# Last output tile stored in two halves on two queues; the first chunk's operand steps put on odd units of the last attention heads

## The chip, the cores and the metric

The program runs on one core of a Trainium2 chip. The metric is the device time of one execution in microseconds (us). The engines of the core are TensorE (PE, with its weight loads PEld), VectorE (DVE), ScalarE (ACT), GpSimd (POOL) and SyncE (SP, which here issues nearly all DMAs). Each has its own instruction queue, taken in order; engines meet only at semaphores.

## The reference

```python
q_bits = (q @ proj > 0); k_bits = (k @ proj > 0)          # 6 bits: one bucket per row
scores = where(bucket(q) == bucket(k), 0.125 * q @ k.T, -1e9)
attn = exp(scores - max) / (sum + 1e-9)                    # [4, 8, 768, 768]
x = (attn @ v).transpose(0, 2, 1, 3).reshape(3072, 512)
h = x @ w_in                                               # [3072, 2048]
g = where(h >= 1, h, where(h <= -1, 0, (h + 1) ** 2 / 4))
out = g @ w_out                                            # [3072, 512] f32
```

## The kernel before

All matrix products are done in pieces of reduced precision: an operand x is split into a high part (a cast to fp32r) and a low part (x minus the high part), and three products (high x high, high x low, low x high) are summed. So for every operand there is a cast and a subtraction somewhere.

**Attention** runs 384 units g = 0 to 383: 32 heads, for each two halves of 384 query columns, for each six key blocks j = g % 6. In unit g, `attention` (the loop at its end) issues in this order:

- `s_unit(g)`: two matmuls into a score tile `s` (L350, L351), two exponentials on ACT (L359 the high part `ph`, L364 the full value). The full value goes back into `s`, or for j = 0 and 3 into an SBUF tile `pf`.
- `max_red`: in odd units up to 359, the maximum of a score tile of a later head, on DVE (L314, `nm<-smax`).
- `lo_unit(g-1)`: the low part `pl` of the unit before, on DVE (`pl<-s,ph`) or, for j = 0 and 3, on POOL (`pl<-pf,ph`). All subtractions go through one helper, L39.
- `pv_unit(g-4)`: three matmuls into `o` (L383, L384, L385). L385 is the one that reads `pl`. The key blocks are taken in the order `PV_ORDER` = 1, 2, 0, 4, 5, 3, so the first one of a half reads block 1: unit 370 reads the `pl` of unit 367, unit 376 that of unit 373, unit 358 that of unit 355.
- `max_mm`: in even units up to 358, two matmuls into `smax` (L310). `smax` is one tile, so they wait until the reduction of the pair before has read it.
- the tasks that were put at g in a table (`at(g, fn, ...)`), in the order in which they were put there.

Tasks of the last four heads (units 336 to 383, `g0 = 336`) prepare the feed-forward part. Those of this case:

- `XMaker.make` makes the operand of the first token chunk for four column tiles ct = 0 to 3, in four steps: part 0, L668, `raw = er * sv + raw` on DVE; part 1, L671, `raw = raw * r` on DVE; part 2, L673, the cast to the high part on DVE (`t<-raw`); part 3 the low part on POOL (L39, `t<-raw,t`). The tile `t` of part 2 and 3 lies in SBUF, as `raw` and `er` do.
- `late[n]` casts a staged weight on DVE (L89, `t<-wsq`) and one unit later subtracts on POOL (L39, `t<-wsq,t`); casts stand in units 354, 366, 371 and 376 among others.

**The feed-forward part** follows (`ffn`): products for the hidden values h (L928, L1023) and for the output y (L791), with ACT and DVE for the activation. `flush` copies a finished output tile of 128 x 512 from PSUM to SBUF and stores it by DMA. The last six tiles of the program are stored at the end, one after the other; the very last copy is on DVE (L778), the others on ACT (L780), and all six DMAs are issued by SP (L781).

The order of all instructions is written out by hand; nothing reorders them.

Of the kernel before, what the change touches and what calls it, by code (L numbers as in the profile page):

```python
# [22 lines left out]
P = 128  # L23
# [586 lines left out]
HM = DM // 2  # L610
# [78 lines left out]
def ffn(ctx, tc, wpair, woh, wol, xm, xa, xb, areas, wst, wq, wc, out, prep, post, staged):  # L689
# [3 lines left out]
    nc = tc.nc  # L693
# [73 lines left out]
    ys = {}  # L767

    def flush(c, m):
        r0 = c * CH + m * P  # L770
        n = (c % 2 * 3 + m) % 4 if c > 1 else 0
        if c == 2 * B - 2:
            ot = pcs.rearrange("p k n -> p (k n)")[:, m * DM:(m + 1) * DM]
        else:
            ot = (xp.tile([P, DM], F32, name="ot", bufs=2) if n < 2
                  else sflat[:, (n - 2) * DM:(n - 1) * DM])
        if c == 2 * B - 2 and m == CH // P - 1:
            nc.vector.tensor_copy(out=ot, in_=ys[c][m])  # L778
        else:
            nc.scalar.copy(out=ot, in_=ys[c][m])  # L780
        nc.sync.dma_start(out=out[r0:r0 + P, :], in_=ot)  # L781

    queue = []
# [1 line left out]
    def queue_out(c, f, g, first, last):  # L785

        def mm(m, k):
            if first and m == 0 and k == 0:
                ys[c] = [ps_y.tile([P, 512], F32, name="y") for _ in range(CH // P)]
            g_, w = ((g[0], woh[f]), (g[0], wol[f]), (g[1], woh[f]))[k]  # L790
            nc.tensor.matmul(out=ys[c][m], lhsT=g_[:, m * P:(m + 1) * P], rhs=w, start=(first and k == 0),  # L791
                             stop=(last and k == 2))
            if last and k == 2:
                flush(c, m)
        queue.extend((mm, (m, k)) for m in range(CH // P) for k in range(3))
# [139 lines left out]
    for ct in range(NCT):  # L935
        for part in range(4):
            n = (1, 2, 3, 5)[ct] + (0, 0, 0, 2)[part]
# [4 lines left out]
    for i in range(4):  # L942
        n = 19 + 3 * i
        w_plan(i, n, n + 2, n + 2, (n + 2, n + 2), (n + 3, n + 3), n + 3)
    for i in range(4, NFT // 2):
        n = N1 + NBLK * (i - 4)
# [60 lines left out]
    for k in range(NK):  # L1007
# [10 lines left out]
        n = 0  # L1018
# [12 lines left out]
        elif s == 2:  # L1031
            src, c, f = ps, 0, 0
        elif s == 3:
            nc.vector.tensor_tensor(out=cv, in0=ps, in1=cm, op=ALU.add)
        elif s == 4:
            nc.vector.tensor_tensor(out=cm, in0=ps, in1=cv, op=ALU.add)
            src, c, f = cm, 1, 1
        elif s == 5:
            nc.vector.tensor_tensor(out=cv, in0=cv, in1=ps, op=ALU.subtract)
            src, c, f = cv, 1, 0  # L1040
        else:
            nc.vector.tensor_tensor(out=cu, in0=ps, in1=cu, op=ALU.add)
            src, c, f = cu, 0, 1
# [24 lines left out]
def lsh_attn_ffn(ctx: ExitStack, tc: tile.TileContext, qk, v, pj, cv, w_in, w_out, out):  # L1068
    nc = tc.nc
# [42 lines left out]
    def at(g, fn, *a):  # L1112
        tasks[g].append((fn, a))
# [50 lines left out]
    for ct in range(NCT):  # L1164
        at(g0 + 4 + 4 * ct, load_er, 0, ct)
        at(gx + 4 + 4 * ct, load_er, 1, ct)
        for part, n in enumerate((14, 18, 19, 20)):
            at(g0 + n + 6 * ct, xm.make, 0, ct, part, *xa, (nc.vector, nc.gpsimd))

    for i in (2, 3):  # L1170
# [9 lines left out]
    for i in range(2, NFT):  # L1180
        n = i + NFT - NW1
# [71 lines left out]
```

## Time and profile before

| what | value |
|---|---|
| median of 3 runs | 985.68 us (984.98 to 985.96) |
| profiled execution: time, span | 986.29 us, 984.5 us |
| busy PE, DVE, ACT, POOL | 98%, 81%, 69%, 35% of the span |
| last matmul ends, last copy ends | 980.60, 981.32 us |
| attention's last units (from unit 350) | from 432.30 us; feed-forward from 468.15 us |
| granted TensorE clock | 1.00 in all windows read here |

The span runs from the first to the last instruction of the profiled execution; 1.8 us of its own time lie around it. Times below are microseconds from the start of the span, and durations of single instructions are from that one execution.

### The profile page before, as it was taken

To read this page: it belongs to the slowest core of one execution; us is meant where nothing else is said; L and a number is where in the kernel's file an instruction comes from. 1 tells how busy PE (TensorE), PEld (TensorE's weight loads), DVE (VectorE), ACT (ScalarE), POOL (GpSimd) and SP (SyncE) were. 2 spreads that over 40 slices of the span, in tenths; PEclk is the share of its full clock that TensorE was granted. 3 is DMA by queue.
4 is the path that set the end of the run, shared out by engine and by line. 5 is a ranking of instruction groups with operands and counts; after the bars stand their busy time and mean duration, and the time that the engine had idled before them with its cause. 6 is when DMAs were issued, how large, how long until landed. Compare 5 with 4: busy or idle time off the path is not lost.

```text
span 984.5 us, 15564 instructions
## 1 busy us (share of the span) xinstructions
PE 968.2 (98%) x5047; PEld 891.9 (91%) x5047; DVE 799.5 (81%) x1359; ACT 679.3 (69%) x1483; POOL 342.1 (35%) x411
## 2 busy tenths in 40 slices
PE   7999999999999999999999999999999999999998
PEld 5789999999999999999999998888988888988896
DVE  8789999999999999988798887887876777655554
ACT  6779888998999888988655556555564545554444
POOL 7666777778877777766100000000000000000000
PEclk8999999999999999999999999999999999999999
DMA  6654667766656667554496478977449554454431
GB/s 174 177 154 101 174 179 191 199 173 168 177 140 180 173 187 191 136 146 124 127 286 217 118 245 271 299 239 210 118 151 245 147 185 116 130 168 118 115 93 64
DMA packets 94712, 167.55 MB, mean 170 GB/s; under 512 B 13940, under 2 KB 51432, under 8 KB 94632
## 3 DMA queue, kind: packets, MB, share of 16 engines
q1 hardware_dynamic: 94408, 166.56, 59.3%
q8 instruction: 40, 0.66, 0.3%
q14 instruction: 40, 0.33, 0.1%
q10 hardware_dynamic: 224, 0.00, 0.0%
HBM read 106.13 MB, written 33.87 MB: 142 GB/s over the span
## 4 chain that ended last, share of the span: by engine, by line
PE 90%; DVE 5%; ACT 2%; DMA 1%; issue 1%; SPq 0%; DVEq 0%
PE y L791 27%; PE h L1023 18%; PE smax L310 7%; PE h L928 7%; PE o L385 6%; PE s L351 6%; PE o L384 6%; PE o L383 6%; PE s L350 6%; PE o L204 2%; DVE nm L314 2%; DMA vraw<-in_v_dram 1%; DVE pl L39 1%; DMA t<-te 1%; ACT ph L359 0%
## 5 line engine op out<-in xcount | busy, mean ns | idle before, releaser
L359 ACT ACTIVATE ph<-s 128x384 fp32r<-128x384 f32 x380 | 188.1, 495 | 47.5 <-PE s L351 41.8
L314 DVE TENSOR_REDUCE nm<-smax 128x1 f32<-128x768 f32 x189 | 178.9, 947 | 16.2 <-PE smax L310 14.5
L39 POOL TENSOR_TENSOR pl<-pf,ph 128x384 fp32r<-128x384 f32 x128 | 139.0, 1089 | 90.4 <-ACT pf L364 90.1
L756 DVE SCALAR_TENSOR_TENSOR t<-t 128x384 f32<-128x384 f32 x128 | 71.3, 557 | 101.7 <-ACT z L751 101.5
L39 DVE TENSOR_TENSOR pl<-s,ph 128x384 fp32r<-128x384 f32 x256 | 135.5, 544 | 10.2 <-ACT s L364 9.4
L350 PE MATMUL s<-t 128*128 128x384 f32 x384 | 132.6, 345 | 0.0
L385 PE MATMUL o<-pl,va 128*128 128x386 f32 x384 | 130.6, 340 | 0.4 <-DVE pl L39 0.4
L384 PE MATMUL o<-ph,vb 128*128 128x386 f32 x384 | 130.6, 340 | 0.0
L351 PE MATMUL s<-t 128*128 128x384 f32 x384 | 130.3, 339 | 0.2 <-DMA t<-te 0.2
L383 PE MATMUL o<-ph,va 128*128 128x386 f32 x384 | 130.2, 339 | 0.1
L364 ACT ACTIVATE s<-s 128x384 f32<-128x384 f32 x252 | 124.9, 496 | 0.0
L791 PE MATMUL y<-t,ghi 128*128 128x512 f32 x384 | 124.6, 395 | 0.0
L310 PE MATMUL smax<-t 128*128 128x384 f32 x378 | 104.0, 356 | 6.6 <-DVE nm L314 6.1
L750 ACT ACTIVATE t<-h,mh 128x384 f32<-128x384 f32 x56 | 32.6, 581 | 84.4 <-PE h L928 44.3
L310 PEld LDWEIGHTS smax<-t 128*128 128x128 f32 x378 | 65.5, 191 | 23.5 <-DVE nm L314 23.0
L761 ACT CAST ghi<-z 128x384 fp32r<-128x384 f32 x129 | 65.1, 505 | 30.1 <-DVE z L757 26.3
L751 ACT ACTIVATE z<-t,m 128x384 f32<-128x384 f32 x128 | 79.0, 617 | 4.2
L1023 PE MATMUL h<-wbig,t 128*128 128x384 f32 x399 | 81.4, 336 | 0.0
L791 PEld LDWEIGHTS y<-t,ghi 128*128 128x128 f32 x384 | 71.3, 188 | 11.1 <-ACT ghi L761 0.3
L1023 PEld LDWEIGHTS h<-wbig,t 128*128 128x128 f32 x399 | 71.6, 188 | 5.3
L791 PE MATMUL y<-t,glo 128*128 128x512 f32 x192 | 76.0, 396 | 0.0
L791 PE MATMUL y<-woh,glo 128*128 128x512 f32 x192 | 75.7, 394 | 0.2
(181 smaller groups left out, 2092.0 us busy)
## 6 DMA issues: line engine op xcount, KB each, us to landing
t<-wc SPq DMA_DIRECT2D x92, 256.0 KB
t<-t SPq DMA_DIRECT2D x60, 384.0 KB
wraw<-wc SPq DMA_DIRECT2D x76, 256.0 KB
raw<-in_qk_dram SPq DMA_DIRECT2D x15, 768.0 KB
wraw<-in_w_in_dram SPq DMA_DIRECT2D x16, 512.0 KB
wraw<-in_w_out_dram SPq DMA_DIRECT2D x16, 512.0 KB
t<-ed SPq DMA_DIRECT2D x36, 192.0 KB
xd<-xs SPq DMA_DIRECT2D x32, 192.5 KB
```

The source lines that it names most:

```text
L39: eng.tensor_tensor(out=out, in0=a, in1=b, op=ALU.subtract)
L310: nc.tensor.matmul(out=smax[hd][:, hf, 0:HS], lhsT=t2[:, 0, h, i * P:(i + 1) * P], rhs=t2[:, 1, h, hf * HS:(hf + 1) * HS], start=True, sto ...
L314: nc.vector.tensor_reduce(out=nmp(hd)[:, i:i + 1], in_=smax[hd][:, :, 0:HS], axis=AX.XY, op=ALU.max, negate=True)
L350: nc.tensor.matmul(out=ps[:, 0:HS], lhsT=t1[:, 1, h, ks], rhs=t1[:, 0, h, sl], start=True, stop=False)
L351: nc.tensor.matmul(out=ps[:, 0:HS], lhsT=t2[:, 1, h, ks], rhs=t2[:, 0, h, sl], start=False, stop=True)
L359: nc.scalar.activation(out=ph[:, 0:HS], in_=ps[:, 0:HS], func=AF.Exp, scale=SCALE)
L364: nc.scalar.activation(out=pf, in_=ps[:, 0:HS], func=AF.Exp, scale=SCALE)
L383: nc.tensor.matmul(out=o, lhsT=wa, rhs=ph, start=(jj == 0), stop=False)
L384: nc.tensor.matmul(out=o, lhsT=wb, rhs=ph, start=False, stop=False)
L385: nc.tensor.matmul(out=o, lhsT=wa, rhs=pl, start=False, stop=(jj == NJ - 1))
L791: nc.tensor.matmul(out=ys[c][m], lhsT=g_[:, m * P:(m + 1) * P], rhs=w, start=(first and k == 0), stop=(last and k == 2))
L1023: nc.tensor.matmul(out=ps, lhsT=w[:, cs], rhs=x, start=(n == 0 and s not in (2, 3, 6)), stop=(n == 5), skip_group_check=True)
```

## The change

```diff
         if c == 2 * B - 2 and m == CH // P - 1:
-            nc.vector.tensor_copy(out=ot, in_=ys[c][m])
-        else:
-            nc.scalar.copy(out=ot, in_=ys[c][m])
+
+            for n, q in enumerate((nc.sync, nc.scalar)):
+                sl = slice(n * HM, (n + 1) * HM)
+                nc.vector.tensor_copy(out=ot[:, sl], in_=ys[c][m][:, sl])
+                q.dma_start(out=out[r0:r0 + P, sl], in_=ot[:, sl])
+            return
+        nc.scalar.copy(out=ot, in_=ys[c][m])
         nc.sync.dma_start(out=out[r0:r0 + P, :], in_=ot)
...
-        for part, n in enumerate((14, 18, 19, 20)):
+        for part, n in enumerate((13, 17, 19, 21) if ct else (15, 17, 19, 21)):
             at(g0 + n + 6 * ct, xm.make, 0, ct, part, *xa, (nc.vector, nc.gpsimd))
```

HM is 256. The first edit replaces the last copy of 512 columns by two of 256, and its store by two, the second issued by ACT. The second edit moves steps between units:

| ct | parts 0, 1, 2, 3 before | now |
|---|---|---|
| 0 | 350, 354, 355, 356 | 351, 353, 355, 357 |
| 1 | 356, 360, 361, 362 | 355, 359, 361, 363 |
| 2 | 362, 366, 367, 368 | 361, 365, 367, 369 |
| 3 | 368, 372, 373, 374 | 367, 371, 373, 375 |

On DVE in units 353 to 357 (here `raw` and `t2_1_78` are the operand's tiles, `wsq` the staged weight; lines with + are of the changed kernel, lines with - of the kernel before, which alone has the rows so marked):

```order
+L671 TENSOR_TENSOR raw_5434<-raw_5434,t2_1_78 128x384
 L39 TENSOR_TENSOR pl_3_164<-s_5637,ph_3_157 128x384
 L89 CAST t1_1_75<-wsq_5593 128x512
-L671 TENSOR_TENSOR raw_5434<-raw_5434,t2_1_78 128x384
-L314 TENSOR_REDUCE nm_5586<-smax_5661 128x1
+L314 TENSOR_REDUCE nm_5586<-smax_5662 128x1
 L673 CAST t2_1_78<-raw_5434 128x384
+L668 SCALAR_TENSOR_TENSOR raw_5434<-t2_1_78,xsv0_5435,raw_5434 128x384
 L39 TENSOR_TENSOR pl_5_166<-s_5666,ph_5_159 128x384
-L668 SCALAR_TENSOR_TENSOR raw_5434<-t2_1_78,xsv0_5435,raw_5434 128x384
-L314 TENSOR_REDUCE nm_5586<-smax_5687 128x1
+L314 TENSOR_REDUCE nm_5586<-smax_5688 128x1
```

Part 1 of ct 0 has moved ahead of the low part of unit 353 and of the weight's cast; part 0 of ct 1 now stands right behind part 2 of ct 0 and ahead of `pl_5_166`, the low part of unit 355. Between the two reductions stand the same three operations as before.

On DVE in units 365 to 369 (`pl_1_162` is the low part of unit 365, `pl_3_164` that of unit 367, `pl_4_165` that of unit 368):

```order
+L671 TENSOR_TENSOR raw_5434<-raw_5434,t2_1_78 128x384
 L39 TENSOR_TENSOR pl_1_162<-s_5788,ph_1_155 128x384
 L89 CAST t1_2_76<-wsq_5749 128x512
-L671 TENSOR_TENSOR raw_5434<-raw_5434,t2_1_78 128x384
 L673 CAST t2_1_78<-raw_5434 128x384
+L668 SCALAR_TENSOR_TENSOR raw_5434<-t2_1_78,xsv0_5435,raw_5434 128x384
 L39 TENSOR_TENSOR pl_3_164<-s_5815,ph_3_157 128x384
-L668 SCALAR_TENSOR_TENSOR raw_5434<-t2_1_78,xsv0_5435,raw_5434 128x384
-L39 TENSOR_TENSOR pl_4_165<-s_5826,ph_4_158 128x384
+L39 TENSOR_TENSOR pl_4_165<-s_5827,ph_4_158 128x384
```

Part 1 of ct 2 goes ahead of the low part of unit 365, and part 0 of ct 3 goes ahead of the low part of unit 367, which it followed before.

## Rows read from the trace of the kernel before

**Rows 1.** Page, part 1: busy time, share of the span, instructions

```profile
PE 968.2 (98%) x5047; PEld 891.9 (91%) x5047; DVE 799.5 (81%) x1359; ACT 679.3 (69%) x1483; POOL 342.1 (35%) x411
```

**Rows 2.** Timeline of PE: start us, duration us, instruction, [idle before <-releaser]

```profile
441.65 0.34 PE L385 MATMUL o<-pl,va 128*128 128x386 f32 x1
442.31 0.61 PE L310 MATMUL smax<-t 128*128 128x384 f32 x2 [0.33 <-DVE nm L314]
...
453.27 0.34 PE L384 MATMUL o<-ph,vb 128*128 128x386 f32 x1
453.45 0.34 PE L385 MATMUL o<-pl,va 128*128 128x386 f32 x1
...
458.68 0.34 PE L384 MATMUL o<-ph,vb 128*128 128x386 f32 x1
459.38 0.44 PE L385 MATMUL o<-pl,va 128*128 128x386 f32 x1 [0.37 <-DVE pl L39]
```

**Rows 3.** Timeline of DVE, units 354 to 357

```profile
437.80 0.41 DVE L89 CAST t<-wsq 128x512 fp32r<-128x512 f32 x1
438.13 0.55 DVE L671 TENSOR_TENSOR raw<-raw,t 128x384 f32<-128x384 f32 x1
...
439.47 0.35 DVE L673 CAST t<-raw 128x384 fp32r<-128x384 f32 x1
...
440.20 1.19 DVE L668 SCALAR_TENSOR_TENSOR raw<-t,xsv,raw 128x384 f32<-128x384 f32 x1
441.32 0.94 DVE L314 TENSOR_REDUCE nm<-smax 128x1 f32<-128x768 f32 x1
```

**Rows 4.** Timeline of POOL, units 354 to 373

```profile
438.30 1.27 POOL L39 TENSOR_TENSOR pl<-pf,ph 128x384 fp32r<-128x384 f32 x1 [2.19 <-ACT pf L364]
439.52 1.45 POOL L39 TENSOR_TENSOR t<-wsq,t 128x512 fp32r<-128x512 f32 x1
...
450.79 1.27 POOL L39 TENSOR_TENSOR pl<-pf,ph 128x384 fp32r<-128x384 f32 x1 [1.96 <-ACT pf L364]
452.02 1.40 POOL L39 TENSOR_TENSOR t<-wsq,t 128x512 fp32r<-128x512 f32 x1
...
456.05 1.29 POOL L39 TENSOR_TENSOR t<-wsq,t 128x512 fp32r<-128x512 f32 x1 [0.37 <-PE s L351]
```

**Rows 5.** Timeline of DVE, units 366 to 372

```profile
450.63 0.55 DVE L671 TENSOR_TENSOR raw<-raw,t 128x384 f32<-128x384 f32 x1
451.22 1.06 DVE L673 CAST t<-raw 128x384 fp32r<-128x384 f32 x1
452.20 0.55 DVE L39 TENSOR_TENSOR pl<-s,ph 128x384 fp32r<-128x384 f32 x1
452.67 1.18 DVE L668 SCALAR_TENSOR_TENSOR raw<-t,xsv,raw 128x384 f32<-128x384 f32 x1
...
456.36 1.40 DVE L671 TENSOR_TENSOR raw<-raw,t 128x384 f32<-128x384 f32 x1
```

**Rows 6.** Line L668: duration ns min/median/max, first and last start

```profile
L668 DVE SCALAR_TENSOR_TENSOR pcs<-t,xsva,pcs x4: 609/610/611, 475.1 to 486.4; 128x384 f32<-128x384 f32 x4
```

**Rows 7.** Timelines at the end: DVE's last copy, SP's last DMA issue

```profile
980.63 0.69 DVE L778 COPY pcs<-y 128x512 f32<-128x512 f32 x1 [3.36 <-PE y L791]
...
981.35 0.33 SPq L781 DMA_DIRECT2D out_dram<-pcs  x1
```

**Rows 8.** Windows at the end: length, busy per engine, PEclk, DMA share, GB/s

```profile
978.50:982.00 3.50, 2.10 (x10) 1.35 (x8) 0.69 (x1) 1.76 (x3) 0.00 (x0) 1.00 0.98 363
982.00:983.00 1.00, 0.00 (x0) 0.00 (x0) 0.00 (x0) 0.00 (x0) 0.00 (x0) 1.00 0.82 301
```

**Rows 9.** Waits of SP's queue after 980: us in total, times, longest

```profile
SPq L1249 <- DMA out_dram<-pcs: 1.7, 1, 1.7
```

**Rows 10.** Timeline of ACT's first microseconds: a DMA it issues, who waits

```profile
0.72 0.41 ACTq L440 DMA_DIRECT2D pj_raw<-in_pj_dram  x1
...
3.43 0.41 ACT L461 CAST pw<-pj_raw 64x6 fp32r<-64x6 f32 x2 [0.78 <-DMA pj_raw<-in_pj_dram]
```

## Prediction

> **What bounds the kernel now.** I read the page first: PE is busy 98% of the span, so time is gained or lost only where PE stands still or behind its last matmul [rows 1]. Then I listed the waits of PE in the stretch of the second edit (units 350 to 383) and followed each in the timelines of PE, DVE and POOL; last came the timeline and the windows of the final five microseconds.
>
> PE's matmuls of attention start 0.18 us apart when nothing waits (453.27, 453.45). Two places break that spacing [rows 2]. At 442.31 the maximum's matmuls of unit 358 start 0.66 us behind the matmul ahead of them and wait for DVE's reduction: 0.48 lost. At 459.38 L385 of unit 376 starts 0.70 behind its predecessor and waits for a low part on DVE: 0.52 lost. So about 1.0 us is all that better placed steps can give back here.
>
> Why DVE is late there: L668 takes 0.61 us in the feed-forward part, where POOL does nothing [rows 6], but 1.19 and 1.18 us here [rows 3, 5]. It ends 0.42 and 0.43 us behind the end of a POOL subtraction that was running when it began: 441.39 behind 440.97, 453.85 behind 453.42 [rows 3 to 5]. L671 shows the same: 0.55 us at 450.63, but 1.40 at 456.36, which ends at 457.76, 0.42 behind the POOL subtraction begun at 456.05 [rows 4, 5]. These DVE operations read and write SBUF alone, and POOL holds them up until it is through. The low parts `pl<-s,ph` read one operand from PSUM, and the one at 452.20 kept its 0.55 us beside a POOL subtraction begun at 452.02 [rows 4, 5]. The other way round, a POOL operation that comes up while DVE has such a one waits for that, and then goes ahead of DVE's next: L671 began at 450.63, POOL at 450.79, and L673 at 451.22 lasted until 452.28, 0.22 behind POOL's end at 452.06 [rows 4, 5]. So the second edit removes no work; it changes which POOL operation each step meets, and what stands behind it in DVE's queue while it is held.
>
> **Units 353 to 358 (term A).** Between the reductions of units 355 and 357 the same three operations stand as before, L673, the low part of unit 355, L668, but the low part is now last. Before, it ran at full speed between 439.47 and 440.20, while POOL had the port from 439.52 to 440.97 and L668 could only wait [rows 3, 4]. Now L668 comes up directly behind L673, finds the same POOL subtraction already waiting, and again ends near 441.39; the low part and then the reduction come behind it. A low part takes 0.55 us and lets the next start after 0.47 (DVE's overlap of about 0.08). So the low part ends near 441.87, where its reader L385 is due at 441.65 [rows 2]: 0.2 lost there. The reduction starts 0.47 us later than 441.32, and the matmuls of unit 358 follow 0.47 us later. The 0.2 lies inside the 0.47. A = +0.5 us.
>
> Bounds: if DVE keeps the port for the pair L673, L668, L668 ends by 439.8 + 0.61 = 440.4, the low part runs to 440.9, the reduction from there to 441.8 is in time, and the 0.48 is gone: A = -0.5. Part 1 of ct 0, moved ahead, pushes the weight's cast from 437.80 to 438.27, and POOL's subtraction begins at 438.30 [rows 3, 4]: if POOL is first, the cast waits for it until about 439.5 instead of ending at 438.7, and the reduction of unit 355 is 0.8 later, with some slack ahead of PE. So A may reach +0.9.
>
> **Units 365 to 371 (term B).** Nothing is lost there to speak of before. Now part 0 of ct 3 stands ahead of the low part of unit 367, the first that L385 of unit 370 reads, due at 453.45 [rows 2]. The cast of the weight takes the place of L671 near 450.7; POOL's subtraction of 450.79 runs to about 452.06 as before, L673 ends at 452.28, POOL's next holds the port from then to 453.42, and L668 ends at 453.85, wherever behind L673 it queued [rows 4, 5]. Before, the low part of unit 367 had slipped in between them at 452.20. Now it follows L668: 453.77 to 454.3, and PE waits for it from 453.45, 0.87 us, with a few hundredths of restart. B = +0.9. Bounds: 0, if L668 is not held (452.28 + 0.61 = 452.9, low part at 453.4); 1.05, if POOL begins its second subtraction only at 452.28 and runs 1.30. I take the row.
>
> **Units 371 to 376 (term C).** Part 1 of ct 3 goes ahead of the low part of unit 371, from 456.36 to about 455.9, in front of POOL's 456.05 [rows 4, 5]. It then takes 0.55 instead of 1.40; L673 behind it meets POOL until about 457.6 and ends near 457.9, so the low part of unit 373 is ready by 458.5 for a reader due at 458.86. The wait of 0.52 goes: C = -0.5. Bounds: -0.6 with the restart, 0 if POOL begins first. What is late next is nothing: behind unit 376 no step of the operand but POOL's own is left.
>
> ct 1 to ct 2 (units 359 to 363) I cost at nothing: between POOL's operations there DVE has room; what it costs if that room is gone is the third rival. The moved steps issue no DMA and pass none on SP or POOL; POOL's part 3 comes one unit later at ct 0, 1, 2, 3 and its product is not read before 468.15.
>
> **The last tile (term D).** The DMA engines are busy 98% from 978.5 to 982 and move 363 GB/s; 363 x 3.5 + 301 = 1571 KB up to 983 is the six tiles of 262 KB [rows 8]. So five tiles are through at about 982.1, and only the last one, issued at 981.35 [rows 7], moves its bytes from 982.1 to about 982.95. Half a copy takes 0.41 us, an estimate from 0.69 for 512 columns [rows 7] and 0.55 for 384 [rows 3]. So the first half is issued near 981.07, 0.28 earlier, and finds the engines still full; the second near 981.5, 0.15 later than the whole before. At 363 GB/s the two halves need 0.72 from 982.1: 982.82. D = -0.1, at best -0.2.
>
> The trace shows full DMA engines at a time when one queue alone feeds them. The Trainium skill, page "DMA: Bandwidth & Descriptors", section "Issuing engines are not separate DMA queues", says that DMAs of all engines share the same 16 DMA engines and that issuing from a second engine saves only the issue itself. By that rule D would be the issue time alone, about what I take.
>
> Upper bound of D: ACT's first DMA took 2.71 us from issue to its reader (0.72 to 3.43) [rows 10]; SP's last was waited for 1.7 us after its issue, that is 2.05 from 981.35, to 983.4 [rows 7, 9]. If the second half takes 2.71 from 981.5, it lands at 984.2: D = +0.8.
>
> **The sum**: +0.5 + 0.9 - 0.5 - 0.1 = +0.8 us. The profiled execution's own 986.29 (span 984.5) becomes 987.1; the runs' median lies 0.6 below that execution, so 985.68 + 0.8 = 986.5.
>
> **The rivals.**
> 1. *The waits go.* DVE keeps the port over two steps in a row, so that the pairs L673, L668 pass before POOL: A = -0.5, B = 0, C = -0.5, D = -0.15: 984.5. For it: these pairs have no dependence on one another, so the second is ready the moment the first ends; L671 and L673 at 450.63 had one. Against: that one case went to POOL.
> 2. *One of the two pairs is held, not the other*, or L668 meets POOL later: between -0.4 and +0.3, say 985.6.
> 3. *Slower.* The pair that moved at ct 1 to ct 2 is held too: L668 in unit 361 loses to POOL's part 3 and ends over a microsecond later, and the low part of unit 361 behind it makes PE wait about 0.6, as in A; A is at 0.9, B at 1.05, and C stays because POOL is first there too. It decides when POOL comes up before L668 at all three pairs. +2.6: 988.2.
> 4. *The second queue lands late*, D = +0.8 with the rest of the forecast: 987.4.
>
> **How the numbers follow.** Forecast 50%, rival 1 22%, rival 2 18%, rival 3 6%, rival 4 4%. The forecast's own range is 985.7 to 987.4 (A and B at their bounds, and half a microsecond of spread between runs). The range 984.5 to 987.5 cuts off half of rival 1 and all of rival 3, 17%. A measurement of this kernel tells 0.2%, 1.97 us, from no change: faster is below 983.7, slower above 987.65. Faster needs more than all the waits of the stretch and the tail together: 3%. Slower is rival 3 and a little of 4 and the forecast's edge: 6%. Within: 91%.
>
> **What would show it.** A right: the L310 of unit 358 still waits for `nm`, by about 1 us, and L668 right behind L673 lasts over 1 us. B right: a new wait of about 0.9 us of L385 in unit 370 for `pl` on DVE, behind an L668 of over 1.5 us. C right: no wait at unit 376, L671 there at 0.55. D right: last bytes at 982.8 relative to a last matmul at 980.6. Wrong: L668 of 0.6 us behind L673, and no wait of PE in units 358 and 370.

## The result, and the profile after

| | before | after |
|---|---|---|
| median of 18 runs each | 985.71 us (984.89 to 987.10) | 987.31 us (986.35 to 989.45) |
| ratio after / before | | 1.0018 [1.0011, 1.0026] |
| profiled execution: time, span | 986.29, 984.5 us | 987.12, 985.3 us |
| unit 350 to the feed-forward part | 35.85 us | 36.62 us |
| last matmul's end to the span's end | 3.91 us | 4.28 us |

The time rose by 1.6 us by the medians and 1.8 us by the ratio, just under the 0.2% that the prediction took for no change. The interval lies wholly above 1, so the change is slightly slower. The profiled execution took 0.8 us more.

The busy row answers to [rows 1]: still 98% of PE, and one DVE instruction more, the second half copy.

```profile
PE 969.4 (98%) x5047; PEld 892.8 (91%) x5047; DVE 799.0 (81%) x1360; ACT 679.4 (69%) x1483; POOL 341.5 (35%) x411
```

**Where PE waits now.** The timeline of PE after, to set beside [rows 2] (start, duration, instruction, idle time before it and what ended that):

```profile
439.17 0.34 PE L385 MATMUL o<-pl,va 128*128 128x386 f32 x1
440.09 0.62 PE L310 MATMUL smax<-t 128*128 128x384 f32 x2 [0.59 <-DVE nm L314]
...
442.12 0.34 PE L385 MATMUL o<-pl,va 128*128 128x386 f32 x1
442.65 0.62 PE L310 MATMUL smax<-t 128*128 128x384 f32 x2 [0.19 <-DVE nm L314]
...
453.64 0.34 PE L384 MATMUL o<-ph,vb 128*128 128x386 f32 x1
454.62 0.44 PE L385 MATMUL o<-pl,va 128*128 128x386 f32 x1 [0.64 <-DVE pl L39]
```

Take the distance between starts, less the usual 0.18: unit 356 loses 0.74, which is new; unit 358 loses 0.35, where it lost 0.48; unit 370 loses 0.80, which is new. The wait of unit 376 is gone, and so is its 0.52.

**What made DVE late.** The timeline of DVE after, for units 351 to 361 and 366 to 372, beside [rows 3, 5]:

```profile
434.76 1.45 DVE L668 SCALAR_TENSOR_TENSOR raw<-t,xsv,raw 128x384 f32<-128x384 f32 x1
436.13 0.94 DVE L314 TENSOR_REDUCE nm<-smax 128x1 f32<-128x768 f32 x1
...
438.40 0.77 DVE L89 CAST t<-wsq 128x512 fp32r<-128x512 f32 x1
439.09 0.94 DVE L314 TENSOR_REDUCE nm<-smax 128x1 f32<-128x768 f32 x1
439.95 0.78 DVE L673 CAST t<-raw 128x384 fp32r<-128x384 f32 x1
440.66 0.61 DVE L668 SCALAR_TENSOR_TENSOR raw<-t,xsv,raw 128x384 f32<-128x384 f32 x1
...
445.85 1.38 DVE L668 SCALAR_TENSOR_TENSOR raw<-t,xsv,raw 128x384 f32<-128x384 f32 x1
...
451.36 1.18 DVE L673 CAST t<-raw 128x384 fp32r<-128x384 f32 x1
452.46 1.64 DVE L668 SCALAR_TENSOR_TENSOR raw<-t,xsv,raw 128x384 f32<-128x384 f32 x1
454.02 1.01 DVE L39 TENSOR_TENSOR pl<-s,ph 128x384 fp32r<-128x384 f32 x2
...
456.41 0.55 DVE L671 TENSOR_TENSOR raw<-raw,t 128x384 f32<-128x384 f32 x1
```

And the timeline of POOL after, beside [rows 4]:

```profile
434.78 1.01 POOL L39 TENSOR_TENSOR pl<-pf,ph 128x384 fp32r<-128x384 f32 x1 [1.15 <-ACT pf L364]
437.86 1.03 POOL L39 TENSOR_TENSOR pl<-pf,ph 128x384 fp32r<-128x384 f32 x1 [2.06 <-ACT pf L364]
439.25 1.27 POOL L39 TENSOR_TENSOR t<-wsq,t 128x512 fp32r<-128x512 f32 x1 [0.36 <-DVE t L89]
440.81 1.32 POOL L39 TENSOR_TENSOR t<-raw,t 128x384 fp32r<-128x384 f32 x1 [0.29 <-DVE t L673]
...
452.28 1.40 POOL L39 TENSOR_TENSOR t<-wsq,t 128x512 fp32r<-128x512 f32 x1
```

In units 366 to 370 it went as forecast: L668 came up behind L673, POOL's 452.28 held it until 0.42 behind its own end (453.68 to 454.10), and the low part that unit 370 reads came at 454.02.

In units 351 to 357 it did not. L668 behind L673, at 440.66, took its undisturbed 0.61 [rows 6]. The loss began earlier, with part 0 of ct 0, which the change put into unit 351: recorded at 434.76, 0.02 ahead of POOL's low part at 434.78, it nevertheless lasted until 436.21, 0.42 behind POOL's end at 435.79. The reduction behind it then started at 436.13, the cast of the weight at 438.40 met POOL's 437.86 and took 0.77 instead of 0.41 [rows 3], and the reduction that unit 356 waits for started at 439.09. Before, the same step stood one unit earlier and 1.67 us ahead of POOL's operation at 435.10, as the timelines of DVE and of POOL before have it. It was held there too, by the subtraction of 432.66, but only until 434.38 (again 0.42 behind POOL's end), and no matmul waited for it:

```profile
433.43 0.95 DVE L668 SCALAR_TENSOR_TENSOR raw<-t,xsv,raw 128x384 f32<-128x384 f32 x1
434.30 0.94 DVE L314 TENSOR_REDUCE nm<-smax 128x1 f32<-128x768 f32 x1
```

```profile
432.66 1.30 POOL L39 TENSOR_TENSOR t<-wsq,t 128x512 fp32r<-128x512 f32 x1
...
435.10 1.01 POOL L39 TENSOR_TENSOR pl<-pf,ph 128x384 fp32r<-128x384 f32 x1 [1.14 <-ACT pf L364]
```

**The end.** The timeline after, beside [rows 7]:

```profile
980.65 0.40 PE L795 MATMUL y<-woh,glo 128*128 128x512 f32 x1
981.09 0.75 DVE L781 COPY pcs<-y 128x256 f32<-128x256 f32 x2 [3.35 <-PE y L795]
981.54 0.33 SPq L782 DMA_DIRECT2D out_dram<-pcs  x1
981.87 0.38 ACTq L782 DMA_DIRECT2D out_dram<-pcs  x1
```

The windows after, beside [rows 8]:

```profile
982.00:983.00 1.00, 0.00 (x0) 0.00 (x0) 0.00 (x0) 0.00 (x0) 0.00 (x0) 1.00 1.02 357
983.00:984.00 1.00, 0.00 (x0) 0.00 (x0) 0.00 (x0) 0.00 (x0) 0.00 (x0) 0.53 0.35 116
```

The last matmul ends 0.45 later than before (981.05 against 980.60). In the trace the last DMA packet of the output ends at 983.43, 2.38 behind that matmul; before it ended at 983.03, 2.43 behind. (The 0.82 and 0.35 of the last windows are busy shares, not the time at which the last byte is through.) So the bytes are through slightly earlier, and what is later is the program's closing, the instructions put down to the file's last line. First those of before (operation, count, shortest/median/longest ns, first and last start), then those of after:

```profile
L1249 SPq EVENT_SEMAPHORE  x7: 17/28/28, 983.4 to 984.4; - x7
L1249 POOLq EVENT_SEMAPHORE  x4: 17/17/17, 983.8 to 984.4; - x4
L1249 SPq DRAIN  x3: 7/7/8, 983.7 to 984.3; - x3
```

```profile
L1253 SPq EVENT_SEMAPHORE  x8: 17/28/28, 983.1 to 985.3; - x8
L1253 POOLq EVENT_SEMAPHORE  x4: 17/17/17, 984.7 to 985.2; - x4
L1253 SPq DRAIN  x3: 7/7/116, 984.2 to 984.9; - x3
```

SP has one semaphore instruction more, one of its drains lasts 116 ns instead of 7, and POOL, which goes on behind SP's drains, does so about 3.65 behind the last matmul's end (984.7 less 981.05) instead of 3.2.

### The profile page after: what moved, and what is told of

Read it like the earlier page. It is cut to its first block, busy times and chain, and to the rows that moved or that the text cites. A ratio compares the mean times of both kernels' runs of the same rounds, so it can differ in the third digit from the quotient of the medians.

```text
span 985.3 us, 15571 instructions
## 1 busy us (share of the span) xinstructions
PE 969.4 (98%) x5047; PEld 892.8 (91%) x5047; DVE 799.0 (81%) x1360; ACT 679.4 (69%) x1483; POOL 341.5 (35%) x411
## 4 chain that ended last, share of the span: by engine, by line
PE 91%; DVE 4%; DMA 2%; ACT 1%; issue 1%; POOL 0%; SPq 0%; DVEq 0%
PE y L795 27%; PE h L1027 18%; PE smax L310 7%; PE h L932 7%; PE o L385 6%; PE o L383 6%; PE o L384 6%; PE s L351 6%; PE s L350 6%; PE o L204 2%; DVE nm L314 2%; DMA vraw<-in_v_dram 1%; DMA t<-te 1%; DMA sm<-sd 0%; DVE pl L39 0%
```

## The experiments

Times in us; "stretch" is from unit 350's first matmul to the feed-forward part (35.85 before, 36.62 after), "tail" from the last matmul's end to the span's end (3.91 and 4.28). Tails here are read to a hundredth; those named in the expectations were worked out from spans rounded to a tenth and are up to 0.05 off.

| kernel | time | ratio to before | stretch | tail |
|---|---|---|---|---|
| the steps alone | 986.67 | 1.0011 [1.0002, 1.0019] | 36.61 | 3.90 |
| the tail alone | 986.65 | 1.0004 [0.9995, 1.0013] | 35.84 | 4.29 |
| halves, both on SP | 985.83 | 0.9999 [0.9991, 1.0008] | 35.84 | 4.14 |
| whole tile on ACT's queue | 986.85 | 1.0003 [0.9992, 1.0014] | 35.86 | 3.92 |
| steps, ct 3's part 0 back | 985.43 | 0.9995 [0.9985, 1.0006] | 35.75 | 3.90 |
| steps, ct 0's part 0 back | 987.47 | 1.0013 [1.0003, 1.0023] | 36.37 | 3.91 |
| steps, POOL's subtraction later | 986.41 | 1.0004 [0.9994, 1.0014] | 35.98 | 3.90 |
| other places for two steps | 985.0 | 0.9988 [0.9979, 0.9997] | 34.74 | 3.91 |
| one copy, row halves, SP and ACT | 987.11 | | 35.81 | 4.57 |
| one copy, column halves, SP and ACT | 986.38 | | 35.84 | 3.98 |
| one copy, row halves on SP | 987.60 | | 35.84 | 5.20 |
| two copies, one store | 988.06 | | 35.84 | 4.39 |

The last four are single executions without a ratio (986.07 for the kernel before beside them); they are read for the tail alone. The stretch repeats within 0.05 wherever the steps are the same, so it tells differences that the runs' times cannot.

**The two edits apart.** The table of units alone:

```diff
-        for part, n in enumerate((14, 18, 19, 20)):
+        for part, n in enumerate((13, 17, 19, 21) if ct else (15, 17, 19, 21)):
```

> The second edit alone, the last tile as before. Theory (the steps cost 0.8 us in attention, the last tile 0.35 us behind the last matmul): ratio about 1.0008 to 1.0012, +0.8 to +1.2 us, with L310 of unit 356 waiting 0.6 to 0.9 us for the reduction and L385 of unit 370 waiting 0.8 us for a low part. Rival (the last tile's two halves carry most of the difference of 1.6 us): under +0.5 us.

It has the changed kernel's three waits (units 356, 358 and 370: idle 0.57, 0.18 and 0.64) and its stretch, and none of its tail: 1.0011.

The other edit alone, the halves in `flush`:

> The first edit alone, the steps where they were. Theory: +0.3 to +0.5 us, from the last matmul to the span's end 4.25 us (before 3.9), data of the last tile through 0.1 us earlier, the end of the wait for the stores 0.4 us later. Rival (only the steps cost time): 0 to -0.2 us.

The stretch is that of before, the tail 4.29: 1.0004, which the runs cannot tell from nothing. SP's wait for the stores does not end 0.4 later, as was expected: it ends 2.76 behind the last matmul, against 2.80 before, and the time goes behind it (see "The tail once more"). The two edits add up to 1.0015, inside the interval of the change's 1.0018.

**Which half of the tail.** The halves with both stores on SP, then the whole tile stored by ACT:

```diff
-            for n, q in enumerate((nc.sync, nc.scalar)):
+            for n, q in enumerate((nc.sync, nc.sync)):
```

> The last tile in two halves, but both stores issued by SP; steps as before. Theory (a store issued by ACT completes later): from the last matmul to the span's end 3.8 us, -0.1 us against before. Rival (two stores of half the size cost a later completion whoever issues them): 4.2 us, +0.3 us.

```diff
-        nc.sync.dma_start(out=out[r0:r0 + P, :], in_=ot)
+        q = nc.scalar if c == 2 * B - 2 and m == CH // P - 1 else nc.sync
+        q.dma_start(out=out[r0:r0 + P, :], in_=ot)
```

> The last tile whole, one copy as before, its one store issued by ACT instead of SP; steps as before. Theory (a store issued by ACT completes later): from the last matmul to the span's end 4.2 to 4.4 us, +0.3 to +0.5 us. Rival (the halves are the cause): 3.9 us, no change.

With a whole store by ACT the last packet ends 0.05 later behind the last matmul than with one by SP (2.48 against 2.43), and the program 0.02 later; tails of the same code lie between 3.90 and 3.91. So the theory that ACT's store lands late fell, and with it the fourth rival. The halves cost 0.2 on SP alone as well.

**ct 3's part 0 back in unit 368** (the rest of the steps as changed; this and the next three kernels have the tail of before):

```diff
-        for part, n in enumerate((13, 17, 19, 21) if ct else (15, 17, 19, 21)):
+        for part, n in enumerate(((15, 17, 19, 21), (13, 17, 19, 21), (13, 17, 19, 21), (14, 17, 19, 21))[ct]):
```

> The second edit alone, but part 0 of column tile 3 back in unit 368, behind the low part of unit 367. Theory (in unit 370 PE waits because the low part of unit 367 stands behind an L668 that POOL holds up): no wait of L385 near 454 us, L668 there still over 1.1 us, feed-forward starts 0.8 to 0.9 us earlier after unit 350 than with all steps moved; the waits of L310 in units 356 and 358 stay. Rival (DVE simply has too much work there): the wait stays or comes one unit later.

The wait of unit 370 is gone. Its timeline of DVE has the low part in front of L668 again, which is held as before the change and keeps nobody waiting:

```profile
451.90 1.18 DVE L673 CAST t<-raw 128x384 fp32r<-128x384 f32 x1
453.00 0.54 DVE L39 TENSOR_TENSOR pl<-s,ph 128x384 fp32r<-128x384 f32 x1
453.47 1.18 DVE L668 SCALAR_TENSOR_TENSOR raw<-t,xsv,raw 128x384 f32<-128x384 f32 x1
```

From unit 365 to the feed-forward part it takes 19.12, the steps alone 19.97, the kernel before 19.87. So B is worth 0.85 and C -0.75.

**POOL's subtraction of the cast of unit 366 put from 367 to 370**, DVE's order as changed:

```diff
-        conv(g0 + g, late[n], (0, 5, 6))
+        conv(g0 + g, late[n], (0, 5, 9 if g == 25 else 6))
```

> The second edit alone with DVE's order untouched; only POOL's subtraction of the weight cast in unit 366 is put in unit 370 instead of 367. Theory (POOL's operation holds L668): L668 near 452.5 us takes 0.6 to 0.7 us instead of 1.64 and the wait of L385 in unit 370 is gone. Rival (the position of the steps on DVE alone makes the wait): L668 may be shorter, but PE still waits over 0.3 us in unit 370.

Its timelines of DVE and of POOL:

```profile
451.66 1.18 DVE L673 CAST t<-raw 128x384 fp32r<-128x384 f32 x1
452.75 0.61 DVE L668 SCALAR_TENSOR_TENSOR raw<-t,xsv,raw 128x384 f32<-128x384 f32 x1
453.28 1.01 DVE L39 TENSOR_TENSOR pl<-s,ph 128x384 fp32r<-128x384 f32 x2
```

```profile
451.51 1.11 POOL L39 TENSOR_TENSOR pl<-pf,ph 128x384 fp32r<-128x384 f32 x1 [2.02 <-ACT pf L364]
452.91 1.33 POOL L39 TENSOR_TENSOR t<-raw,t 128x384 fp32r<-128x384 f32 x1 [0.30 <-DVE t L673]
```

With no POOL operation ready when L668 comes up, it takes 0.61, and PE does not wait. The order on DVE is the changed one, so it is POOL that holds it, not DVE's own load. This is the cleanest of the experiments on B: one POOL instruction moved, 0.65 us back in that part of the stretch (19.32).

**ct 0's part 0 back in unit 350:**

```diff
-        for part, n in enumerate((13, 17, 19, 21) if ct else (15, 17, 19, 21)):
+        for part, n in enumerate(((14, 17, 19, 21), (13, 17, 19, 21), (13, 17, 19, 21), (13, 17, 19, 21))[ct]):
```

> The second edit alone, but part 0 of column tile 0 back in unit 350, between the low part of unit 349 and the reduction of unit 351. Theory (the wait of unit 356 comes from L668 in unit 351, which comes up 0.02 us ahead of a POOL subtraction, is held 1.45 us and makes everything behind it late): no wait of L310 in unit 356, the one in unit 358 between 0 and 1.0 us, the wait of unit 370 stays at 0.6. Rival (the pair L673, L668 in unit 355 is the cause): the wait in unit 356 stays.

The wait of unit 356 is gone, so L668 of unit 351 was its cause. But the stretch to unit 365 falls only from 16.64 to 16.39 (15.98 before). Its timelines of PE, DVE and POOL show why:

```profile
440.33 0.62 PE L310 MATMUL smax<-t 128*128 128x384 f32 x2 [0.42 <-DVE nm L314]
```

```profile
437.02 0.35 DVE L673 CAST t<-raw 128x384 fp32r<-128x384 f32 x1
437.29 1.65 DVE L668 SCALAR_TENSOR_TENSOR raw<-t,xsv,raw 128x384 f32<-128x384 f32 x1
438.87 0.54 DVE L39 TENSOR_TENSOR pl<-s,ph 128x384 fp32r<-128x384 f32 x1
439.33 0.94 DVE L314 TENSOR_REDUCE nm<-smax 128x1 f32<-128x768 f32 x1
```

```profile
437.07 1.46 POOL L39 TENSOR_TENSOR t<-wsq,t 128x512 fp32r<-128x512 f32 x1
```

Here the forecast's A happens as it was worked out: the subtraction of 437.07, recorded 0.05 behind L673, goes ahead of L668 and holds it until 0.41 behind its own end, and the low part and the reduction come behind. In the changed kernel L668 came up at 440.66, when POOL's subtraction of 439.25 had ended (440.52) and its next one still waited for L673: the delay from unit 351 had moved it past that meeting.

**Other places for two steps.** Part 0 of ct 1 goes from unit 356 to 359, where it is clear of the pair, and parts 1 to 3 of ct 3 stand in 371, 373 and 375 as in the changed kernel; all else is as before the change:

```diff
-        for part, n in enumerate((14, 18, 19, 20)):
+        for part, n in enumerate(((14, 18, 19, 20), (17, 18, 19, 20), (14, 18, 19, 20), (14, 17, 19, 21))[ct]):
```

> Last tile as before; of the steps only these are moved: part 0 of column tile 1 from unit 356 to 359, behind the last reduction, and parts 1 to 3 of column tile 3 to 371, 373, 375 as in the changed kernel. Theory: the waits of units 358 and 376 are both gone and no new one comes, -1.0 to -1.2 us against before (ratio 0.999). Rival (POOL holds a step at its new place too): a new wait of 0.3 us or more, and no gain that can be told.

The profile lists no wait of PE for DVE in the stretch any more: 34.74 instead of 35.85. The runs give 0.9988 against the kernel before, less than the 0.2% named above, though the interval keeps clear of 1.

**The tail once more: pieces, stores or copies?** Before these four the question was whether the 1 KB pieces of a column half or the second completion cost the time. Column halves after one whole copy:

```diff
+            nc.vector.tensor_copy(out=ot, in_=ys[c][m])
             for n, q in enumerate((nc.sync, nc.scalar)):
                 sl = slice(n * HM, (n + 1) * HM)
-                nc.vector.tensor_copy(out=ot[:, sl], in_=ys[c][m][:, sl])
                 q.dma_start(out=out[r0:r0 + P, sl], in_=ot[:, sl])
```

> One copy of 512 columns, then two column halves (1 KB pieces) on SP and ACT, both ready at the same time. If the size of the pieces or the two stores cost the time, 4.2 to 4.4 from the last matmul to the end. If it was the second half's later issue (0.15 us behind the whole copy), 4.0 to 4.1.

Two stores of 1 KB pieces on two queues, and a tail of 3.98: not the 4.2 to 4.4 of pieces or completions, and just under the 4.0 to 4.1 of a second half that is only issued later. The reverse, two half copies and one whole store by SP:

> Two half copies by DVE, then one whole store by SP. The second copy ends about 0.07 to 0.15 us later than one whole copy did; the store follows that: 3.95 to 4.05 if the copies count, 3.88 to 3.95 if the DMA engines are full until then and hide it.

4.39, above both of its expectations and the longest of these, though it stores as the kernel before does. The closing of the two kernels, first column halves after one copy, then two copies with one store:

```profile
L1252 SPq EVENT_SEMAPHORE  x7: 17/28/28, 983.5 to 984.5; - x7
...
L1252 SPq DRAIN  x3: 7/7/8, 983.8 to 984.4; - x3
```

```profile
L1253 SPq EVENT_SEMAPHORE  x8: 17/28/28, 984.0 to 986.2; - x8
...
L1253 SPq DRAIN  x3: 7/7/117, 985.1 to 985.8; - x3
```

Of these two kernels the one with two copies has the long drain and the eighth semaphore, so the second store isn't needed for them. Read instruction by instruction, SP's last wait for a DMA begins to clear 2.80 behind the last matmul's end before, 2.75 after, 2.76 with the tail alone, 2.87 with column halves after one copy, 2.86 with two copies and one store; from there to the end it is 1.11 before and with one copy, 1.53 in the other three. So the data are in by nearly the same time, and SP's closing is 0.42 longer. In the trace SP has 1106 instructions before and with one copy, 1107 in the three; and in those three a pause of 0.35 stands between its 1103rd and 1104th, in front of the long drain. With the halves both on SP there are 1109, and the pause stands between the same two numbers, there in front of a semaphore. So it does with row halves on SP alone (1107, below), which has one copy: what the five kernels with the pause share is more instructions on SP than before, not the two copies. No DMA packet is in flight during the pause in any of the five. Before, the 1103rd is the drain that lets POOL go, and SP's next 0.37 is spent waiting for the others anyway.

Row halves of 64 rows, on SP and ACT and on SP alone:

```diff
+            for n, q in enumerate((nc.sync, nc.scalar)):
+                sl = slice(n * 64, (n + 1) * 64)
+                q.dma_start(out=out[r0 + n * 64:r0 + (n + 1) * 64, :], in_=ot[sl])
```

> The last tile is copied whole as before; its store goes out as two of 64 rows each (2 KB pieces), on SP and ACT. Read is the stretch from the end of the last matmul to the end of the span: 3.88 to 3.95 us in six profiles with one whole store by SP, 4.25 and 4.33 with two column halves on SP and ACT. If two completions, or the second queue beside the first, cost the time: 4.2 to 4.4. If the 1 KB pieces of the column halves cost it: 3.8 to 4.0.

> One copy, two stores of 64 rows each (2 KB pieces), both issued by SP one after the other. Column halves on SP took 4.11 to 4.14. If the second issue on SP (0.4 us later) and a second completion cost the 0.2: 4.1 to 4.2 again. If the 1 KB pieces cost it: 3.85 to 4.0.

4.57 and 5.20, above either expectation, and mostly for another cause, the bytes themselves: the last packet ends 3.10 and 3.38 behind the last matmul, 0.67 and 0.95 later than before. The other 0.34 of the second kernel is its closing, which has the pause. The windows of the first of the two:

```profile
982.00:983.00 1.00, 0.00 (x0) 0.00 (x0) 0.00 (x0) 0.00 (x0) 0.00 (x0) 1.00 0.56 158
983.00:984.00 1.00, 0.00 (x0) 0.00 (x0) 0.00 (x0) 0.00 (x0) 0.00 (x0) 1.00 0.69 197
```

The DMA engines are 0.56 busy in the first window, where one store of 128 rows kept them at 0.82 [rows 8], and have 0.69 of the next one left to do. The Trainium skill, page "DMA: Bandwidth & Descriptors", section "Rules for kernel authors", advises against two transfers to disjoint partition halves, because they share the same engines. The trace agrees that nothing is won, and shows tails that are 0.7 and 1.3 us longer.

## Why the prediction was right, and where not

The forecast was 986.5 with a range of 984.5 to 987.5 and 91% for no change; 987.31 lies inside, and 0.16% is no change by the bound named there. But the way to it differs in two of four terms.

- **A, +0.5: size about right, place wrong.** From unit 350 to unit 365 the change costs 0.68 (15.98 to 16.66). The step that failed is that part 0 of ct 0 was given no cost: the table of moved steps has it from 350 to 351, and the prediction went through the units from 353 on. It meets POOL's low part of unit 350 there, and PE waits 0.74 for what comes of it. The step that was worked out, L668 held behind L673 in unit 355, did not occur in the changed kernel: L668 took 0.61 there, and unit 358 lost 0.35, not about 1. It occurs, at +0.41, once part 0 of ct 0 is put back. The first pushed L668 past the second, so the two costs do not add, and that 0.68 came near +0.5 is luck. In A's bounds the cast of the weight held by POOL was named as the way to +0.9; the cast was held (0.77), as a part of this chain.
- **B, +0.9: right,** in place, mechanism and size: 0.80 of wait, 0.85 with its restart. L668 lasted 1.64 where "over 1.5" was called for, and moving one POOL subtraction takes the wait away.
- **C, -0.5: right,** the wait of unit 376 is gone, L671 takes 0.55 at 456.41; with small gaps around it -0.75.
- **ct 1 to ct 2 at nothing: right.** L668 of unit 361 was held, 1.38 us at 445.85, and no matmul waited: the third rival had the hold and not the wait.
- **D, -0.1: wrong in sign.** The transfer did about as forecast: its last packet and the end of SP's wait came about 0.05 earlier behind the last matmul. (The 982.95 that the forecast counted from stands in none of its rows, whose 0.82 would give 982.82 and D nothing; the trace has 983.03.) The step that failed is that what follows the last byte was taken as fixed: SP's closing got one instruction more and became 0.42 longer. No row of the kernel before shows that price. Rival 4 had the sign and not the cause. The +2.6 of rival 3 leaves D out; with it, it is +2.45.

The second rival's condition, one of the two pairs held and not the other, is what the trace shows; its 985.6 fell by the cost in unit 351. By the profiles the stretch gives +0.77 and the tail +0.38, in all +1.15 against a sum of +0.8; between the two, from the feed-forward part to the last matmul, both kernels take 512.45. The runs' +1.6 is 0.45 above that. It isn't located: ahead of unit 350 all these kernels are the same, and yet its first matmul starts anywhere from 429.32 to 433.61 in the single profiled executions; +1.15 lies near the lower end of the ratio's interval.

Left open is what SP's pause of 0.35 is. That it stays between the same two instruction numbers in five kernels speaks for a place in SP's instruction stream and against any transfer; a kernel that adds one instruction to SP and nothing else was not run.

## What to carry to other kernels

Where two engines compete for SBUF, cost every moved instruction by what the other engine starts within about a microsecond of it, including the first one of the table and those that move by a single unit; the operation that PE then waits for can stand right behind the held one (unit 370) or six places further on in the queue (unit 356). POOL did not hold the low parts that read PSUM (of the 140 on DVE that ran beside a subtraction on POOL before the change, none took over 0.56 us), so putting one in front of an SBUF-only step shields its reader, as in unit 368 with ct 3's part 0 put back. At the end of a program look at the closing instructions as well as at the last byte: here they cost 0.42 us, more than the 0.1 to 0.2 that the transfer was to win.

## What was not expected of the hardware

- A DVE operation recorded 0.02 us ahead of a POOL operation was the one that waited (434.76 against 434.78, end 0.42 behind POOL's). The Trainium skill, page "SBUF — State Buffer", section "Who interferes with whom", says that a DVE instruction with two SBUF inputs contends with a GpSimd instruction that reads SBUF, and that issue order decides who blocks. The hold is as it says (L668 ended 0.42 behind POOL's end in units 351 and 367, 0.41 with ct 0's part 0 put back); either two recorded starts this close do not tell who was first, or being first by so little is not enough, and no run here shows which.
- With one instruction more on SP a pause of 0.35 us stands in the open, where before a wait of 0.37 stood at the same place, and the program's closing is 0.42 longer. That the count alone does it was not tested.
- A store of 128 x 512 split by rows on two queues was through 0.67 us later than the whole one (last packet 3.10 behind the last matmul against 2.43); split by columns after one copy, 0.08 (2.51).
